# Transposes of two finished tiles in every second step, with three places for keys and x

## The chip, the cores and the metric

The kernel runs on one core of a Trainium2 chip, in one launch. The metric is the device time of one execution in microseconds (us). The kernel before takes 389.77 us, the median of three runs (389.64 to 392.35).

## The reference, cut to what matters

```
# retention attention: batch 8, heads 8, sequence 576, head size 64
scores = q @ k.T / sqrt(64)
Dmat   = where(rel >= 0, gamma[h] ** rel, 0)        # rel = row - column
attn   = (scores * Dmat) @ v
x      = attn, one row a token: 4608 x 512
# mixture of experts on x: 8 experts, hidden size 1024
do     = x @ w_skip > 0
e      = argmax(x[do] @ w_gate);  g = softmax(...)[e]
y      = g * (relu(x @ w1[e]) @ w2[e])              # one expert a token
out    = x;  out[do] = x[do] + y
```

Each token's output is its x, plus the result of one expert where `do` holds.

## The kernel before, in words

The first part of the kernel is a loop over 36 tiles of 128 tokens (`for g in range(NT)`, lines 856 to 888). Nine tiles make a pair of batch entries; the ninth holds the last 64 tokens of both. A tile's q, k, v and a second form of k come as two loads of 512 KB each (`load_half`, on SP's queue), into one of five buffers `u`. The second part (`experts`) runs the experts on gathered rows; it begins with the first lead expert, for which tiles are counted and gathered while the last steps of the loop still run.

The order of TensorE's instructions is the order of the source (a manual schedule for this engine). The other engines' orders are chosen by a planner from its own costs, apart from instructions that are pinned: `tc.keep_in_program_order` holds an instruction behind the one traced before it on its engine.

One step g holds, in this order:

- **Scores** of tile g + 1 (`scores`, line 571), on TensorE tiles of 64x64, and between them the products of masked scores and v of tile g - 1 (`second`, line 662). A tile's scores have two parts: `psc`, the near part, in bank `sc0` or `sc1` by the parity of the tile, and `psq`, the far part, in the one bank `sc2`.
- **Masks** of tile g + 1 (`decay`, lines 586 to 593): one VectorE product for the far part, one for the near part of each half of the partitions, and for each half a ScalarE copy of the rest of the near part. They read the banks and write `sq` and `u`.
- **Keys** of tile g + 2 and **value rows** of tile g + 1 (`keys`, line 601, and `rows_of`, line 623), on GpSimd. The keys `kn` have two places.
- Once in four steps (g = 5, 9, ...) the **gate logits** of four tiles (`logits_a`, line 712), and in the step after it their transposes into bank `xn` (`logits_b`, line 727). VectorE then computes the gates of a group of tiles (`route_a`).
- **State and values** (lines 637 and 686), on TensorE tiles of 128x64. VectorE multiplies the result into `xt` (line 698).
- **Turning a finished tile** (`stage_c`, lines 700 to 707): four transposes of tile g - 2 on TensorE, in tiles of 128x128, into the one bank `xn`; a ScalarE copy to `xn` in SBUF, which has two places; and a DMA to `out`, issued on ScalarE's queue.
- **Routing** (`routing`, line 800): it adds the slot matches of the step before on TensorE (`slot_add`, line 277), and then takes up to three pieces of a list: `route_b` (ranks of a group of tiles; one short set of products, then small VectorE operations) or the slot match of one tile (line 272, VectorE). A piece is due only from a given step. From step 28 up to eight pieces are taken.

Pools give each name a number of places (`bufs`); an instruction that writes a place waits until its last reader is done. The pool `ap` has two unless a call says otherwise.

Of the kernel before, what the change touches and what calls it, by code (L numbers as in the profile page):

```python
# [11 lines left out]
F32 = mybir.dt.float32  # L12
# [5 lines left out]
ALU = mybir.AluOpType  # L18
# [3 lines left out]
B, H, S, D = 8, 8, 576, 64  # L22
NTOK, DM, NE, DF = B * S, H * D, 8, 1024
P = 128
NT = NTOK // P
HALF = S // P * 2
NQ = HALF + 1
NPR = H // 2
# [24 lines left out]
GROUPS = (8, 8, 8, 4, 4, 4)  # L53
KONE = 2
QD = 32
NQD = P // QD
KCUT = 3
KRANK = 4
KFRONT = 1
KCOUNT = 3  # L60
# [27 lines left out]
def kernel(  # L88
# [9 lines left out]
    nc = tc.nc  # L98
# [28 lines left out]
    nc.gpsimd.iota(iota, pattern=[[P, NBLK], [1, P]], base=0, channel_multiplier=0, allow_small_or_imprecise_dtypes=True)  # L127
    desc = const.tile([P, NE], F32, tag="desc", name="desc")
    nc.gpsimd.iota(desc, pattern=[[-1, NE]], base=NE, channel_multiplier=0, allow_small_or_imprecise_dtypes=True)
    pidx = const.tile([P, NT], F32, tag="pidx", name="pidx")  # L130
    nc.gpsimd.iota(pidx, pattern=[[0, NT]], base=0, channel_multiplier=1, allow_small_or_imprecise_dtypes=True)
    tidx = const.tile([P, NT], F32, tag="tidx", name="tidx")
    nc.gpsimd.iota(tidx, pattern=[[1, NT]], base=1, channel_multiplier=0, allow_small_or_imprecise_dtypes=True)
    ones = const.tile([P, P], BF16, tag="ones", name="ones")
# [81 lines left out]
    starts = np.cumsum((0,) + GROUPS).tolist()  # L216
# [4 lines left out]
    def route_b(ps, first, late, pin, n, t0, ex, mb):  # L221
        c0 = NE * NCMP * NBLK + t0 * NE
        pr = ps[:, c0 : c0 + n * NE]

        nc.tensor.matmul(pr, utri, mb, start=first, stop=False, skip_group_check=True)
        if t0:
            nc.tensor.matmul(
                pr, ones, cbs[t0].unsqueeze(1).broadcast_to([P, n, NE]), start=False, stop=False, skip_group_check=True
            )
        for t in range(n - 1):  # L230
            nc.tensor.matmul(
                pr[:, (t + 1) * NE :],
                ones,
                mb[:, t : t + 1, :].broadcast_to([P, n - 1 - t, NE]),
                start=False,
                stop=t == n - 2,
                skip_group_check=True,
            )
        if first:
            nc.vector.tensor_copy(cp[:, :, 1], pidx[:, : max(GROUPS)])  # L240
            tile_numbers(t0, n)
        sm = rt.tile([P, n], F32, tag="sm", name=f"sm_{t0}")
        add = nc.vector.tensor_reduce(sm, ex, axis=AX.X, op=ALU.add)
        if pin:
            tc.keep_in_program_order(add)
        nc.vector.reciprocal(cp[:, :n, 2], sm)
        for k in (2, 3):
            gb = rt.tile([P, n], BF16, tag="gb", name=f"gb_{t0}_{k}")
            nc.vector.tensor_copy(gb, cp[:, :n, k])
            nc.vector.tensor_tensor(cp[:, :n, k + 1], cp[:, :n, k], gb, ALU.subtract)  # L250
        nc.vector.tensor_tensor(
            mc[:, t0 : t0 + n, :].rearrange("p t (e k) -> p t e k", k=NCMP),
            mb.unsqueeze(3).broadcast_to([P, n, NE, NCMP]),
            cp[:, :n].unsqueeze(2).broadcast_to([P, n, NE, NCMP]),
            ALU.mult,
        )
        prv = pr.rearrange("p (t e) -> p t e", e=NE)
        if late:
            nc.vector.tensor_tensor(prv, prv, bump.unsqueeze(1).broadcast_to([P, n, NE]), ALU.add)
        mk = rt.tile([P, n, NE], F32, tag="mk", name=f"mk_{t0}")  # L260
        nc.vector.tensor_tensor(mk, prv, mb, ALU.mult)
        nc.vector.tensor_reduce(trank[:, t0 : t0 + n], mk, axis=AX.X, op=ALU.add)
        if t0 + n < NT:
            tile_numbers(t0 + n, GROUPS[starts.index(t0 + n)])
# [227 lines left out]
    with ExitStack() as actx:  # L492
# [88 lines left out]
        def decay(g):  # L581

            q = first(g)
            near, far = psc_t.pop(g)
            sc_t[g] = ap.tile([P, NPR, D], F32, tag="sq", name=f"sq_{g}", bufs=2 + LAG)
            nc.vector.tensor_tensor(sc_t[g], far, dq_sb[:, g % NQ // 2], ALU.mult)
            for j in range(2):
                h = halves[1 - j]
                nc.vector.tensor_tensor(  # L589
                    u_t[g][h, j, :, :D], near[h, :, :D], mt_sb[h].unsqueeze(1).broadcast_to([D, NPR, D]), ALU.mult  # L590
                )
                if q.stop > D:
                    nc.scalar.copy(u_t[g][h, j, :, D:], near[h, :, D:])  # L593

        def keys(g):
            i = g % NQ
            if i == HALF:
                return
            kn_t[g] = ap.tile([P, NPR, P], F32, tag="kn", name=f"kn_{g}")
            k = TK + i // 2 * 2  # L600
            nc.gpsimd.tensor_tensor(  # L601
                kn_t[g].rearrange("p a (j i) -> p a j i", j=2),
                u_t[g][:, 3].rearrange("p a (j i) -> p a j i", j=2),
                tt_sb[:, k : k + 2, :].rearrange("p j a -> p a j").unsqueeze(3).broadcast_to([P, NPR, 2, D]),
                ALU.mult,
            )
# [93 lines left out]
        def stage_c(g, tag="xn"):  # L700
            b, o = divmod(g, NB)
            px = pp.tile([P, DM], F32, tag=tag, name=f"px_{g}")
            for c in range(NCC):
                nc.tensor.transpose(px[:, c * P : (c + 1) * P], xt_t[b][:, c, o * P : (o + 1) * P], ident)
            xn = ap.tile([P, DM], F32, tag="xn", name=f"xn_{g}")
            nc.scalar.copy(xn.rearrange("t (p c) -> t p c", c=NCC), px.rearrange("t (c p) -> t p c", c=NCC))
            nc.scalar.dma_start(out[g * P : (g + 1) * P, :], xn)

# [147 lines left out]
        for g in range(NT):  # L856
            ahead = g + 1 < NT
            last = g - LAG
            products = [scores(g + 1)] if ahead else []
            if last >= 0 and last % NQ < HALF:  # L860
                products.append(second(last))
            in_turn(*products)
            if g and g + UAHEAD - 1 < NT:
                load_half(g + UAHEAD - 1, 2, last_product())
            if last >= 0 and last % NQ == HALF:
                in_turn(second(last))
            if ahead:
                decay(g + 1)
            if g == 0:
                rows_of(1)  # L870
            if g + 2 < NT:
                keys(g + 2)
            if g and ahead:
                rows_of(g + 1)
            if g + 1 < len(NKEEP):
                keep_up(NKEEP[g + 1])
            if g < NQ - 1 and g % 2 == 0:
                table(g // 2 + 1)
            elif g < NQ - 1:
                growth(g // 2 + 1)  # L880
            logits(g)
            in_turn(state(g), *([values(last)] if last >= 0 else []))
            if g + UAHEAD < NT:
                load_half(g + UAHEAD, 0)
            if last >= 1:
                stage_c(last - 1)
            routing(0 if g == NT - 1 else 3 if g < starts[KCUT + 1] else 8)
            weights()
        g = NT
        if LAG:  # L890
# [520 lines left out]
```

## Time and profile before

| what | value |
|---|---|
| median of three runs | 389.77 us |
| the profiled execution | 392.81 us, span 391.1 us |
| TensorE (PE) busy | 369.3 us, 94% |
| VectorE (DVE) busy | 275.5 us, 70% |
| ScalarE (ACT) busy | 181.4 us, 46% |
| GpSimd (POOL) busy | 149.1 us, 38% |
| moved by DMA | 106.15 MB, mean 271 GB/s |

Busy time is the union of an engine's instructions over the span. TensorE's products are pipelined, so its instructions overlap, and the weight loads (PEld) run beside the products. The loop over tiles lies between some 5 and 152 us. Times within the trace count from the start of the span. A wait is put down to what ended it; "issue" means that nothing that the profile shows ended it.

### The profile page before, as it was taken

How to read it: one execution, taken by the hardware profiler on the slowest of the kernel's cores; microseconds unless marked ns; L12 is line 12 of the kernel's file. 1: busy time of each engine (PE TensorE's matmuls, PEld its weight loads, DVE VectorE, ACT ScalarE, POOL GpSimd, SP SyncE). 2: the span in 40 equal slices, each digit the busy share in tenths (PEclk: the TensorE clock that was granted, in tenths of full speed). 3: DMA queues.
4: the chain of work that ended last, by engine and by line, in shares of the span. 5: the costliest groups of instructions: out<-in, count | busy, mean ns of one | idle time of the engine just before them, and what ended most of it. 6: DMA issues, size and time to landing. Idle time of an engine off the chain costs nothing. (4 is left out here: it accounts for less than half of the span.)

```text
span 391.1 us, 12327 instructions
## 1 busy us (share of the span) xinstructions
PE 369.3 (94%) x4884; PEld 335.0 (86%) x4886; DVE 275.5 (70%) x615; ACT 181.4 (46%) x369; POOL 149.1 (38%) x211
## 2 busy tenths in 40 slices
PE   7889999989998989999999999999999999999992
PEld 3758777777886967888899999999999999999992
DVE  3665688568577886876856767857877877687763
ACT  2444555444544567215544545453645536554311
POOL 5875674564555589451134100520320421002032
PEclk9999999999999999999999999999999999999998
DMA  8997998999899896346896987869979998886511
GB/s 306 405 345 233 385 330 309 321 323 329 288 341 340 293 400 219 129 102 212 287 274 193 355 255 271 295 185 358 255 229 376 270 281 306 272 279 219 160 67 61
DMA packets 49573, 106.15 MB, mean 271 GB/s; under 512 B 6102, under 2 KB 21206, under 8 KB 49511
## 3 DMA queue, kind: packets, MB, share of 16 engines
q1 hardware_dynamic: 40951, 85.81, 65.6%
q0 software_dynamic: 3232, 9.99, 7.9%
q10 hardware_dynamic: 5328, 9.52, 6.4%
q8 instruction: 40, 0.66, 0.7%
q14 instruction: 22, 0.18, 0.1%
HBM read 83.51 MB, written 22.28 MB: 271 GB/s over the span
## 5 line engine op out<-in xcount | busy, mean ns | idle before, releaser
L170 DVE TENSOR_TENSOR wlo_w<-w,whi_w 128x1024 fp32r<-128x1024 f32 x59 | 72.0, 1223 | 36.7 <-ACT whi_w L169 33.7
L169 ACT CAST whi_w<-w 128x1024 fp32r<-128x1024 f32 x59 | 61.8, 1050 | 34.6 <-PE py L464 29.3
L464 PE MATMUL py<-hlo,whi_w 128*128 128x336 f32 (+6 forms) x224 | 67.8, 303 | 0.2 <-DVE hlo L473 0.2
L464 PE MATMUL ph<-xhi,wlo_w 128*128 128x336 f32 (+6 forms) x224 | 67.6, 302 | 0.0
L464 PE MATMUL ph<-xlo,whi_w 128*128 128x336 f32 (+6 forms) x224 | 67.5, 302 | 0.0
L464 PE MATMUL ph<-xhi,whi_w 128*128 128x336 f32 (+6 forms) x224 | 67.5, 301 | 0.0
L464 PE MATMUL py<-hhi,wlo_w 128*128 128x336 f32 (+6 forms) x224 | 67.5, 301 | 0.0
L464 PE MATMUL py<-hhi,whi_w 128*128 128x336 f32 (+6 forms) x224 | 67.4, 301 | 0.0
L1032 POOL DMA_INDIRECT out<-rs,sidx x17 | 21.2, 1247 | 85.5 <-DVE rs L1031 78.8
L601 POOL TENSOR_TENSOR kn<-u,tab_sb 128x512 f32<-128x512 f32 x32 | 34.1, 1067 | 46.1 <-DMA u<-qkv 27.3
L623 POOL TENSOR_TENSOR vs<-u,tab_sb 64x256 f32<-64x256 f32 x72 | 45.2, 628 | 10.6 <-DMA u<-qkv 2.8
L686 PE MATMUL pxt<-u,vs 128*64 128x128 f32 (+1 forms) x576 | 47.8, 269 | 1.2 <-issue 1.1
L589 DVE TENSOR_TENSOR u<-psc,tab_sb 64x256 f32<-64x256 f32 x72 | 30.3, 420 | 24.9 <-PE pxt L662 8.7
L593 ACT COPY u<-psc 64x256 f32<-64x256 f32 x64 | 23.4, 366 | 50.9 <-DVE u L589 46.3
L472 ACT ACTIVATE hhi<-ph 128x336 fp32r<-128x336 f32 (+8 forms) x61 | 25.8, 423 | 43.2 <-PE ph L464 34.8
L464 PEld LDWEIGHTS py<-hlo,whi_w 128*128 128x128 f32 x224 | 42.2, 188 | 0.7 <-DVE hlo L473 0.7
L464 PEld LDWEIGHTS ph<-xhi,whi_w 128*128 128x128 f32 x224 | 42.3, 189 | 0.1
L464 PEld LDWEIGHTS ph<-xlo,whi_w 128*128 128x128 f32 x224 | 42.3, 189 | 0.1
L464 PEld LDWEIGHTS py<-hhi,whi_w 128*128 128x128 f32 x224 | 42.3, 189 | 0.0
L464 PEld LDWEIGHTS ph<-xhi,wlo_w 128*128 128x128 f32 x224 | 42.3, 189 | 0.0
L464 PEld LDWEIGHTS py<-hhi,wlo_w 128*128 128x128 f32 x224 | 42.3, 189 | 0.0
L571 PE MATMUL psc<-u 64*64 64x128 f32 (+1 forms) x576 | 39.9, 272 | 1.3 <-issue 0.9
(213 smaller groups left out, 779.4 us busy)
## 6 DMA issues: line engine op xcount, KB each, us to landing
u<-qkv SPq DMA_DIRECT2D x68, 512.0 KB
w<-w SPq DMA_DIRECT2D x64, 512.0 KB
out<-xn ACTq DMA_DIRECT2D x36, 256.0 KB
hop<-xg SPq DMA_DIRECT2D x12, 256.0 KB
xh<-hop SPq DMA_DIRECT2D x48, 64.0 KB
hopy<-yp SPq DMA_DIRECT2D x24, 128.0 KB
yr<-hopy SPq DMA_DIRECT2D x6, 512.0 KB
u<-qkv SPq DMA_DIRECT2D x4, 256.0 KB
```

Of the source, the lines that this page charges most:

```text
L169: nc.scalar.copy(hi, t)
L170: nc.vector.tensor_tensor(lo, t, hi.bitcast(F32), ALU.subtract)
L464: nc.tensor.matmul(ps, x, y, start=first and n == 0, stop=last and n == 3 * len(terms) - 1)
L472: nc.scalar.activation(hi, ph, AF.Relu)
L571: nc.tensor.matmul(psc_t[g][c][halves[1 - j ^ c], a, : q.stop - q.start], u[halves[j], 1 - j, a, c * D : (c + 1) * D], u[halves[j], j, a, ...
L589: nc.vector.tensor_tensor(u_t[g][h, j, :, :D], near[h, :, :D], mt_sb[h].unsqueeze(1).broadcast_to([D, NPR, D]), ALU.mult)
L593: nc.scalar.copy(u_t[g][h, j, :, D:], near[h, :, D:])
L601: nc.gpsimd.tensor_tensor(kn_t[g].rearrange("p a (j i) -> p a j i", j=2), u_t[g][:, 3].rearrange("p a (j i) -> p a j i", j=2), tt_sb[:, k ...
L623: nc.gpsimd.tensor_tensor(vs_t[g][h, j], u_t[g][h, 2, :, j * D : (j + 1) * D], tt_sb[h, TV + g % NQ // 2, :].unsqueeze(2).broadcast_to([D, ...
L686: nc.tensor.matmul(pxt[halves[j], a, q], vs_t[g][:, j, a, :], u_t[g][:, j, a, q], start=False, stop=a == NPR - 1, skip_group_check=True,)
L1032: done = nc.gpsimd.indirect_dma_start(out=out, out_offset=bass.IndirectOffsetOnAxis(ap=idx, axis=0), in_=rs[:n], in_offset=None, bounds_ch ...
```

## The change

In the steps before step 28, the finished tiles are turned in pairs, in odd steps alone: tile g - 3 by way of bank `xn`, then tile g - 2 by way of bank `sc0`, which is the near scores' bank of the tile whose masks belong to that step (`sc{(g+1)%2}`). Even steps turn none, and route none: routing takes up to four pieces in odd steps. From step 28 all is as before, a tile a step.

The keys and the x copies have three places each. To make room in SBUF, `pidx` has 8 columns and not 36.

All masks are pinned in program order on VectorE. For tiles of even number from 4 to 28 the two near parts come first, one behind the other, and the far part last; for the other tiles the far part comes first. ScalarE's copies are traced behind all of them.

```diff
+NXN = 3
+NKN = 3
...
-    pidx = const.tile([P, NT], F32, tag="pidx", name="pidx")
-    nc.gpsimd.iota(pidx, pattern=[[0, NT]], base=0, channel_multiplier=1, allow_small_or_imprecise_dtypes=True)
+    pidx = const.tile([P, max(GROUPS)], F32, tag="pidx", name="pidx")
+    nc.gpsimd.iota(pidx, pattern=[[0, max(GROUPS)]], base=0, channel_multiplier=1, allow_small_or_imprecise_dtypes=True)
...
-            nc.vector.tensor_tensor(sc_t[g], far, dq_sb[:, g % NQ // 2], ALU.mult)
-            for j in range(2):
-                h = halves[1 - j]
-                nc.vector.tensor_tensor(
-                    u_t[g][h, j, :, :D], near[h, :, :D], mt_sb[h].unsqueeze(1).broadcast_to([D, NPR, D]), ALU.mult
-                )
-                if q.stop > D:
+
+            def far_part():
+                tc.keep_in_program_order(nc.vector.tensor_tensor(sc_t[g], far, dq_sb[:, g % NQ // 2], ALU.mult))
+
+            def near_part():
+                for j in range(2):
+                    h = halves[1 - j]
+                    near_mask = nc.vector.tensor_tensor(
+                        u_t[g][h, j, :, :D], near[h, :, :D], mt_sb[h].unsqueeze(1).broadcast_to([D, NPR, D]), ALU.mult
+                    )
+                    tc.keep_in_program_order(near_mask)
+
+            for part in (near_part, far_part) if g % 2 == 0 and 3 < g <= starts[KCUT + 1] else (far_part, near_part):
+                part()
+            if q.stop > D:
+                for j in range(2):
+                    h = halves[1 - j]
                     nc.scalar.copy(u_t[g][h, j, :, D:], near[h, :, D:])
...
-            kn_t[g] = ap.tile([P, NPR, P], F32, tag="kn", name=f"kn_{g}")
+            kn_t[g] = ap.tile([P, NPR, P], F32, tag="kn", name=f"kn_{g}", bufs=NKN)
...
-            xn = ap.tile([P, DM], F32, tag="xn", name=f"xn_{g}")
+            xn = ap.tile([P, DM], F32, tag="xn", name=f"xn_{g}", bufs=NXN)
...
-            if last >= 1:
+            if g >= starts[KCUT + 1]:
                 stage_c(last - 1)
-            routing(0 if g == NT - 1 else 3 if g < starts[KCUT + 1] else 8)
+                routing(0 if g == NT - 1 else 8)
+            elif last >= 1 and g % 2:
+                stage_c(last - 2)
+                stage_c(last - 1, f"sc{(g + 1) % 2}")
+                routing(4)
```

Here `last` is g - 1 and `starts[KCUT + 1]` is 28.

## Rows read from the trace of the kernel before

**Rows 1.** The page, part 1: busy us (share of the span) and instructions.
```profile
PE 369.3 (94%) x4884; PEld 335.0 (86%) x4886; DVE 275.5 (70%) x615; ACT 181.4 (46%) x369; POOL 149.1 (38%) x211
```

**Rows 2.** Busy time by stretch: steps, end; last granted clock, DMA share, GB/s.
```profile
16.80:116.20 99.40, 92.79 (x2241) 75.67 (x2239) 67.01 (x174) 48.34 (x118) 58.55 (x85) 1.00 0.92 323
...
152.20:391.10 238.90, 231.15 (x1644) 223.88 (x1642) 172.00 (x331) 106.13 (x192) 55.21 (x56) 0.99 0.74 238
```

**Rows 3.** TensorE's waits, 16.8 to 152 us: total us, times, longest us.
```profile
PE psq L571 <- issue: 2.6, 3, 1.6
PE pxt L662 <- issue: 2.2, 3, 1.0
PE pl L712 <- issue: 1.6, 1, 1.6
PE pxt L686 <- issue: 1.1, 1, 1.1
PE pn L727 <- ACT xn L706: 1.0, 2, 0.6
PE psc L571 <- issue: 0.9, 1, 0.9
PE psc L571 <- DMA u<-qkv: 0.2, 1, 0.2
```

**Rows 4.** Waits of SP's queue of loads, 16.8 to 116.2 us.
```profile
SPq L516 <- PE pxt L686: 45.0, 26, 4.3
SPq L516 <- PE pxt L662: 30.9, 22, 2.6
```

**Rows 5.** Timeline of TensorE at 123.7 us: start, us, line, count, idle before.
```profile
123.74 0.27 PE L571 MATMUL psq<-u 64*64 64x64 f32 x1 [1.59 <-issue]
```

**Rows 6.** DMA view, 16.8 to 152 us: queues with packets, MB, share of 16 engines.
```profile
DMA packets 14492, 43.47 MB, mean 321 GB/s; under 512 B 1615, under 2 KB 1615, under 8 KB 14459
...
q10 hardware_dynamic: 4697, 8.57, 16.7%
...
q8 instruction: 24, 0.39, 1.2%
```

**Rows 7.** Timeline of TensorE through one even step, 102.6 to 106 us.
```profile
102.70 0.33 PE L571 MATMUL psc<-u 64*64 64x128 f32 x2
...
103.79 0.34 PE L637 MATMUL ps_s<-u,kn 128*64 128x64 f32 x4
...
104.84 0.29 PE L637 MATMUL ps_s<-u,kn 128*64 128x64 f32 x4
104.96 0.39 PE L686 MATMUL pxt<-u,vs 128*64 128x128 f32 x4
105.28 0.66 PE L704 MATMUL px<-ident,xt 128*128 128x128 f32 x4
105.87 0.27 PE L571 MATMUL psc<-u 64*64 64x64 f32 x2
```

**Rows 8.** Timeline of TensorE: parts of one block of transposes, cut by windows.
```profile
120.42 0.49 PE L704 MATMUL px<-ident,xt 128*128 128x128 f32 x3
...
120.64 0.27 PE L704 MATMUL px<-ident,xt 128*128 128x128 f32 x1
```

**Rows 9.** Timeline of VectorE and ScalarE in the step of rows 7.
```profile
104.35 0.42 DVE L586 TENSOR_TENSOR sq<-psq,dq_sb 128x256 f32<-128x256 f32 x1
...
104.80 0.42 DVE L589 TENSOR_TENSOR u<-psc,tab_sb 64x256 f32<-64x256 f32 x1
...
105.25 0.36 ACT L593 COPY u<-psc 64x256 f32<-64x256 f32 x1 [0.48 <-DVE u L589]
```

**Rows 10.** Timeline of TensorE at 63.3 us.
```profile
63.30 0.66 PE L727 MATMUL pn<-ident,lt 128*128 128x128 f32 x4 [0.58 <-ACT xn L706]
```

**Rows 11.** Waits of GpSimd and ScalarE, 16.8 to 116.2 us.
```profile
POOL kn L601 <- PE ps_s L637: 10.3, 5, 3.4
...
ACT xn L706 <- DMA out<-xn: 1.5, 2, 1.1
```

**Rows 12.** Slot matches: ns shortest, median, longest; first and last start in us.
```profile
L272 DVE TENSOR_SCALAR r<-iota,trank x36: 394/402/414, 59.8 to 165.6; 128x384 bf16<-128x384 f16 x36
```

More of the change, by code (lines that the diff above doesn't have):

```diff
@@ L239, in route_b @@
         if first:
-            nc.vector.tensor_copy(cp[:, :, 1], pidx[:, : max(GROUPS)])
+            nc.vector.tensor_copy(cp[:, :, 1], pidx)
             tile_numbers(t0, n)
```

## The prediction

> **What bounds the kernel now.** I read the page first: TensorE is busy for 94% of the span [rows 1], so what it does or waits for moves the end. Then the stretches: the change touches the steps from 16.8 to 116.2 us (tiles 0 to 25 turned, every mask up to tile 28); there TensorE is busy 92.79 of 99.40 us at a granted clock of 1.00 (the 2.4 GHz level), and the DMA engines show a share of 0.92 [rows 2]. Behind the steps TensorE is busy for 231.15 of 238.90 us: a gain in the steps passes on to the end, if loads and routing keep up, and both are paced by TensorE's steps. Third, what TensorE waited for in the steps. Of 9.6 us in all, 8.4 us are "issue": nine stops that no semaphore ends [rows 3]. Only 1.0 us is a wait for ScalarE's copy of x, 0.6 us of it in the steps that change (the other 0.4 us lies behind them), and 0.2 us a wait for a load. So loads, keys and masks are not what ends TensorE's waits. The loads in turn mostly wait for TensorE to give their buffers back: 45.0 and 30.9 us on the queue of loads [rows 4].
>
> The nine stops stand inside blocks of products. One is the row at 123.74 [rows 5]: in the middle of the scores, 1.59 us without a matmul. Over the steps the instruction queue of the DMA moves 24 packets, 0.39 MB, so 16 KB each [rows 6]. I read a stop as a block of TensorE's code that came late, at the worst of 24 places 1.6 us late.
>
> **The change part by part.**
>
> *Transposes in pairs.* What a block of four transposes costs TensorE is read from the start of it to the start of what follows: 105.28 to 105.87, 0.59 us [rows 7]. Its first one comes 0.32 us after the last group of values (104.96), where the group before it came 0.12 us earlier: TensorE changes from tiles of 128x64 to 128x128, and something is lost there. Four more transposes behind four cost less, as they follow at 0.11 us: three take 0.49 us, the last of them 0.27 us, so (0.49 - 0.27) / 2 [rows 8]. Four of them are 0.44 us. Two blocks cost 2 x 0.59 = 1.18 us before and 0.59 + 0.44 = 1.03 us after: 0.15 us less a pair, provided that scores come behind values, with no transposes between, after the same 0.32 us. No row shows that junction in a full step. Bounds: 0.12 us (no change of tiles at all) makes it 0.35 us a pair; 0.47 us makes the pair worth nothing. I take 0.32, the nearest row, which also ends a block of values. There are 13 pairs (odd steps 3 to 27): 13 x 0.15 = 1.95 us, between 0 and 13 x 0.35 = 4.6 us.
>
> *Their bank.* The second transposes go to the bank of the scores of tile g + 1, and wait for ScalarE's second copy out of it. In the step at 104 that copy starts at 105.25 and takes 0.36, so it ends 0.33 us behind the start of the transposes at 105.28 [rows 9, 7]. The second four start 0.59 us behind the first: 0.26 us of margin. The new order puts both near masks ahead of the far one: the second near mask moves up by one mask, 0.45 us [rows 9], and the margin to 0.7 us. Cost 0; where the cover is gone, TensorE stands for what is missing.
>
> *The wait for x.* The products of the gate logits write the bank of the transposes and once waited 0.58 us for ScalarE's copy, which stood behind a late mask copy [rows 10]. In the even steps, where these products are, there are no transposes now, and the copy of the step before has the scores as cover: 0.6 us less.
>
> *Three places for x.* ScalarE waited 1.5 us in two places for an output to land [rows 11]. With pairs, the second of a pair needs the place of the first of the pair before, two steps earlier, as now. 0.
>
> *Three places for keys.* GpSimd waited 10.3 us in five places for TensorE to give a keys buffer back [rows 11], but TensorE's page of waits has no row for keys in these steps [rows 3]. 0; what would be late next is the second half of the load, which the keys are made from.
>
> *Routing.* It moves from three pieces a step to four in two steps. What goes into a step on VectorE is 0.4 us a slot match [rows 12]; the lists still end before step 28, from which all is as before. The transposes' copies and output DMAs move with them, a step later for half of the tiles, past nothing on SP or GpSimd; on ScalarE's queue two issues follow each other. The masks are now held behind what VectorE was given last, in even steps up to four slot matches, 1.6 us; the next scores, which write the far mask's bank, start 2.6 us behind the scores before them where no transposes lie between (1.09 to the state and values, 1.49 for these [rows 7]). 0.
>
> Sum: 1.95 + 0.6 = 2.5 us off TensorE's own work. Not all of it counts: where a code block is late, TensorE gets there earlier and stands longer. Nine of 24 blocks are late, so I give 9/24 back: 2.5 x 0.375 = 0.9. The sum is **1.6 us less**. The profiled execution took 392.81 us, its span 391.1, so 391.2 for such a one. It lies 3.0 us above the median of 389.77; taken from the median, **388.2 us**.
>
> The Trainium skill, "Runtime: NRT & Kernel Launch", Instruction fetch mechanics, says that the sequencer fetches the next 16 KiB block itself while it executes the current one, and that crossing a boundary is mostly hidden. The block size agrees with the trace's 16 KB [rows 6], the hiding does not in nine places [rows 3]. By that rule nothing would be given back, and the time would be 387.3.
>
> **The rivals.**
>
> *All of it counts*: the nine stops are there for reasons that do not move with TensorE. 389.77 - 2.5 = 387.3. For it: 15 of 24 blocks come in time. Against: a stop that ends with an arrival is not moved by coming to it sooner. What the Trainium skill says above under "Runtime: NRT & Kernel Launch" is this case.
>
> *Stops go as well.* Even steps carry no outputs, so the code comes sooner there; if half of 8.4 us goes and odd steps lose nothing, 2.5 + 4.2 = 6.7 less, 383.1. For it: the outputs take 16.7% of the DMA engines' time in the steps [rows 6]. Against: the same bytes come in the other step.
>
> *The loads take it back.* The loads give nothing if DMA is the pace: 0.92 of it is in use, and a stretch of steps without stops would run into a late load. 389.8. For it: one wait for a load is there already [rows 3]. Against: it is the only one in 135 us, and 0.2 us long.
>
> *Slower: paired outputs hold up code.* Two outputs of 0.26 MB (128 x 512 x 4 bytes) are issued within a microsecond in odd steps. At the 321 GB/s of the steps [rows 6] one more of them is 0.82 us. If it delays the 12 blocks that fall in odd steps by that, each of them late: 12 x 0.82 = 9.8 us, less what even steps get back (half of nine stops, 0.82 each, 3.7 us). 389.77 - 2.5 + 6.1 = 393.4 with the refund and 397.1 without; 395.2 between. It decides from the point where a block comes later than the last instruction before it; nine do now. For it: stops up to 1.6 us beside queues that are 92% full. Against: most blocks come in time next to single outputs.
>
> **How the numbers follow.** The forecast (388.2) gets 0.40, "all of it counts" 0.17, "stops go as well" 0.16, "the loads take it back" 0.16, slower 0.11. One per cent, about what a measurement can tell from no change, is 3.9 us: faster is below 385.9, slower above 393.7. So faster 0.17 (the rival and a tail of the forecast's low bound), slower 0.11, same 0.72. The range: low, it reaches into the faster rival, to 384.0, beyond the forecast's own low bound (4.6 + 0.6 with nothing given back, 384.6); high, past "the loads take it back" to 392.5, since single runs before lie between 389.64 and 392.35. Left out is about half of the faster rival and the slower one, 0.19.
>
> **What would show it.** TensorE's transposes in 13 groups of eight between 20 and 120 us, each pair 1.0 us from its start to the next scores; no row of TensorE waiting for the x copy in the even steps; "issue" waits of TensorE in the steps near 9 us, not 5 or 15. Wrong would be: transposes waiting for ScalarE's copy of u more than a few tenths in all, waits of the scores for loads above 1 us, or stops that differ by several us from 8.4, since that is larger than the whole gain.

## The result and the profile after

The changed kernel takes 393.96 us, the median of 21 runs (389.07 to 398.9); the kernel before takes 390.43 us beside it (21 runs). The ratio is 1.0061 with a 95% interval of 1.0034 to 1.0088: slower by some 2.4 us, where 1.6 us less were forecast. Ratios here and below leave disturbed runs out, so they can differ from the quotient of two medians.

The profiled execution shows little of that. It took 392.55 us (span 390.8), near the span of 391.1 us of before. The page's first part and the two stretches:

```profile
PE 368.0 (94%) x4886; PEld 335.0 (86%) x4886; DVE 276.6 (71%) x615; ACT 180.5 (46%) x369; POOL 150.4 (38%) x211
```
```profile
16.80:116.20 99.40, 91.77 (x2238) 75.63 (x2234) 67.21 (x175) 46.58 (x118) 59.37 (x87) 1.00 0.93 327
152.20:390.80 238.60, 230.19 (x1639) 223.54 (x1639) 172.16 (x330) 105.61 (x190) 56.13 (x56) 0.99 0.73 237
```

TensorE is busy 1.3 us less than before over the span and 1.0 us less in the first stretch [rows 1, 2], and the end has not moved as much. One execution hides the result because stops come and go from run to run: over 16.8 to 152 us, "issue" was 8.4 us in the profile of before [rows 3] and is 3.8 us here, and neither number is the kernel's own (a second profile of each follows below). What is the changed kernel's own is the first row of TensorE's waits from 16.8 to 152 us (total us, times, longest us):

```profile
PE px L716 <- ACT u L605: 3.4, 4, 1.0
PE ps_s L649 <- issue: 1.7, 3, 1.3
...
PE ps_s L649 <- POOL kn L613: 0.8, 1, 0.8
PE px L716 <- DVE lg L740: 0.6, 1, 0.6
...
PE psc L573 <- DMA u<-qkv: 0.5, 1, 0.5
PE pn L739 <- ACT xn L718: 0.5, 1, 0.5
```

Transposes stand four times, 3.4 us, for ScalarE's copy of `u` out of the near scores' bank. No such row was there before [rows 3]. The four places are steps 11, 15, 19 and 27, odd steps all. Step 15 by the timeline of VectorE, ScalarE and TensorE (start, us, engine, line, idle before):

```profile
65.97 0.67 DVE L710 TENSOR_TENSOR xt<-pxt,gt_sb 128x512 f32<-128x512 f32 x1
...
66.56 0.71 DVE L274 TENSOR_SCALAR r<-iota,trank 128x384 bf16<-128x384 f16 x2
...
67.24 0.39 PE L698 MATMUL pxt<-u,vs 128*64 128x128 f32 x4
67.29 0.86 DVE L595 TENSOR_TENSOR u<-psc,tab_sb 64x256 f32<-64x256 f32 x2
67.56 0.66 PE L716 MATMUL px<-ident,xt 128*128 128x128 f32 x4
...
68.23 0.75 ACT L605 COPY u<-psc 64x256 f32<-64x256 f32 x2 [1.62 <-PE px L716]
...
69.03 0.66 PE L716 MATMUL px<-ident,xt 128*128 128x128 f32 x4 [0.81 <-ACT u L605]
```

The scores of the tile are done by 66.0 us. VectorE first finishes `xt` and two slot matches left from earlier steps, so the near masks begin at 67.29. Both copies follow at 68.23, behind both masks, and end at 68.98. The first four transposes start at 67.56, the second four at 69.03: 1.47 us behind them, where they follow after 0.49 us in a pair that doesn't wait. So a wait costs more than its row says. From its start to what follows, this pair takes 1.96 us, and one without a wait, with the same kind of products behind it, 0.93. Worked out in this way, the four waits of 3.4 us cost TensorE 4.3 us.

At the other three places (steps 11, 19 and 27) it is the operations of the gates, not slot matches, that VectorE does ahead of the near masks. Step 19, the longest wait (its second four transposes start at 84.74):

```profile
82.52 0.27 DVE L208 TENSOR_REDUCE cb<-mks 128x8 bf16<-128x64 bf16 x1
...
82.82 0.17 DVE L210 TENSOR_TENSOR cb<-cb,cb 128x8 bf16<-128x8 bf16 x1
83.00 0.86 DVE L595 TENSOR_TENSOR u<-psc,tab_sb 64x256 f32<-64x256 f32 x2
83.06 0.66 PE L716 MATMUL px<-ident,xt 128*128 128x128 f32 x4
```

Where the copies are done in time, a pair goes through as costed:

```profile
101.00 1.09 PE L716 MATMUL px<-ident,xt 128*128 128x128 f32 x8
...
104.50 0.39 PE L698 MATMUL pxt<-u,vs 128*64 128x128 f32 x4
104.82 0.27 PE L573 MATMUL psc<-u 64*64 64x64 f32 x2
```

Eight transposes in one row of 1.09 us, and scores 0.32 us behind the last values of an even step: the junction that no row of before showed costs what was taken for it.

The code's queue has not moved, and the outputs' queue little. Over 16.8 to 152 us (packets, MB, share) they stand beside [rows 6] as

```profile
q10 hardware_dynamic: 4874, 8.88, 18.5%
...
q8 instruction: 24, 0.39, 1.2%
```

### The profile page after: what moved, and what is told of

The parts are those of the page before. It is cut to its first block, busy times and chain, and to the rows that moved or that the text cites. A ratio compares the mean times of both kernels' runs of the same rounds, so it can differ in the third digit from the quotient of the medians.

```text
span 390.8 us, 12339 instructions
## 1 busy us (share of the span) xinstructions
PE 368.0 (94%) x4886; PEld 335.0 (86%) x4886; DVE 276.6 (71%) x615; ACT 180.5 (46%) x369; POOL 150.4 (38%) x211
## 5 line engine op out<-in xcount | busy, mean ns | idle before, releaser
L1048 POOL DMA_INDIRECT out<-rs,sidx x17 | 19.8, 1166 | 85.0 <-DVE rs L1047 83.8
L649 PE MATMUL ps_s<-u,kn 128*64 128x64 f32 x512 | 37.8, 227 | 4.9 <-POOL kn L613 3.2
L649 PEld LDWEIGHTS ps_s<-u,kn 128*64 128x64 f32 x512 | 30.5, 136 | 13.9 <-issue 7.2
```

What stands on the lines that cost most here:

```text
L649: nc.tensor.matmul(ps_s[halves[j], i % 2, a, :], kn_t[g][:, a, j * D : (j + 1) * D], u_t[g][:, 2, a, j * D : (j + 1) * D], start=i == 0 an ...
L1048: done = nc.gpsimd.indirect_dma_start(out=out, out_offset=bass.IndirectOffsetOnAxis(ap=idx, axis=0), in_=rs[:n], in_offset=None, bounds_ch ...
```

## The experiments

Each kernel has its own ratio to the kernel before, from runs on the same chip; kernels told under one heading shared a chip and its runs of the kernel before, unless said otherwise. A table made from the profiles comes last.

### What part of the change costs

Theory M: the new order of the masks is the cause. Its rivals: the pairs, or the places.

Pairs and their routing alone, with the masks and places of before:

```diff
-            if last >= 1:
+            if g >= starts[KCUT + 1]:
                 stage_c(last - 1)
-            routing(0 if g == NT - 1 else 3 if g < starts[KCUT + 1] else 8)
+                routing(0 if g == NT - 1 else 8)
+            elif last >= 1 and g % 2:
+                stage_c(last - 2)
+                stage_c(last - 1, f"sc{(g + 1) % 2}")
+                routing(4)
```

> The kernel before with the pairs of transposes and their routing alone; masks as before, two places for keys and x. Theory M (masks): the changed kernel is slower because the first ScalarE copy out of the scores' bank now waits for both near masks, and the masks stand late on VectorE in odd steps, so that the second four transposes of a pair wait (four waits of 1.0 us in the changed kernel's profile, 4.0 us with one behind the gate logits). With the masks as before the copies run between the masks: waits of the transposes under 1 us in all, and the time is 1 to 2 us below the kernel before. Rival O (outputs): two outputs in one go hold up loads and blocks of code; then this kernel is slower as the whole change is, by 2 to 4 us, with waits for loads or stops without a releaser in place of the waits for ScalarE.

Measured: 392.58 us, ratio 1.0073 (1.0040 to 1.0107).

The places alone (in every kernel with three places of either kind, `pidx` is the short one of the change):

```diff
-            kn_t[g] = ap.tile([P, NPR, P], F32, tag="kn", name=f"kn_{g}")
+            kn_t[g] = ap.tile([P, NPR, P], F32, tag="kn", name=f"kn_{g}", bufs=NKN)
...
-            xn = ap.tile([P, DM], F32, tag="xn", name=f"xn_{g}")
+            xn = ap.tile([P, DM], F32, tag="xn", name=f"xn_{g}", bufs=NXN)
```

> The kernel before with three places for keys and x alone. Theory M: no difference beyond 1 us, as TensorE waited for x once for 0.6 us and never for keys in the steps. Rival O: no difference either. A slowing of 2 us or more would say that keys taken earlier on GpSimd, or the other layout in SBUF, is the cause.

Measured: 392.16 us, ratio 1.0051 (1.0012 to 1.0089).

The masks alone:

```diff
...
+            for part in (near_part, far_part) if g % 2 == 0 and 3 < g <= starts[KCUT + 1] else (far_part, near_part):
+                part()
...
```

> The kernel before with the masks' order and pins alone, and ScalarE's copies traced behind all masks; one block of transposes a step, all in the bank of their own. Theory M: the copies end some 0.4 us later, but the transposes do not use the scores' bank, so 0 to 1 us slower, with no row of transposes waiting for ScalarE's copy of u above a few tenths. Rival O: 0. If this is slower by 2 us or more, the pins cost in themselves, by what they hold up on VectorE.

Measured: 390.09 us, ratio 1.0008 (0.9978 to 1.0037).

Pairs and places together, without the masks (the first two of these diffs):

> The changed kernel with the masks and copies as before: pairs and three places. Theory M: 1 to 2.5 us faster than the kernel before, waits of transposes for ScalarE under 1 us. Rival O: 2 to 4 us slower than the kernel before, as the whole change.

Measured: 394.59 us, ratio 1.0075 (1.0034 to 1.0116).

Theory M fell: the masks alone cost nothing that can be told, and the pairs without them are as slow as the whole. The pairs alone have the changed kernel's wait, at other lines of the source; the pairs with places have less of it (TensorE's waits, 0 to 152 us, of the one and then of the other):

```profile
PE px L704 <- ACT u L593: 2.9, 4, 1.1
PE ps_s L637 <- POOL vs L623: 2.9, 2, 1.6
```
```profile
PE px L706 <- ACT u L595: 1.6, 3, 0.8
```

So theory W took its place: the second four transposes meet ScalarE's late copies, since VectorE has gates and slot matches to do ahead of the masks. Rival O: the outputs, now two close together, hold up code or loads. Pairs with places speak against W as the whole cause: 1.6 us of the wait, and the same 1.0075.

### Taking the wait away, and pairing the outputs alone

The pairs alone, with VectorE's two pieces moved behind the masks (the gates of a group thus a step later):

```diff
...
-            slot_match(t)
+            if g < starts[KCUT + 1]:
+                with tc.issue_after(marks["mask"].ins):
+                    slot_match(t)
+            else:
+                slot_match(t)
...
+            if later:
+                with tc.issue_after(marks["mask"].ins):
+                    route(*later.pop())
             if lt is not None:
                 logits_b(*lt)
-                route(lt[0])
+                if g < starts[KCUT + 1]:
+                    later.append((lt[0], g + 2))
+                else:
+                    route(lt[0])
...
```

> The pairs alone (old masks, old places) with two pieces of VectorE's work moved: the gates of a step are worked out one step later, behind that step's masks, and the slot matches stand behind the masks. Theory W (the second four transposes of a pair wait for ScalarE's copies out of their bank, because VectorE has gates and slot matches to do ahead of the masks): the waits of the transposes for ScalarE, 2.9 us in the pairs alone, fall below 1 us, and the time falls by 2 to 3 us from the 392.6 of the pairs alone, to 389 to 391, ratio to the kernel before 0.997 to 1.003. Rival O (two outputs close behind each other hold up code and loads): the outputs are as close as in the pairs alone, so it is as slow, ratio 1.005 to 1.009, whatever the transposes wait.

Measured: 391.19 us, ratio 1.0027 (0.9990 to 1.0063); TensorE has no wait for ScalarE's copies of `u` any more. Against the pairs alone, which ran on another chip, the ratio is lower by 0.0046, plus or minus 0.0050 (the half-widths joined as roots of squares): in time this run alone doesn't tell W from O.

The kernel before with three places for x and the outputs of two tiles issued together:

```diff
...
+            ready.append((g, xn))
+            if g % 2 or g >= starts[KCUT + 1] - 2:
+                with tc.issue_after(turned.ins):
+                    for t, x in ready:
+                        nc.scalar.dma_start(out[t * P : (t + 1) * P, :], x)
+                ready.clear()
...
```

> The kernel before with three places for x, where the outputs of two tiles are issued together behind the copy of the second, in odd steps; transposes and copies stay single. Rival O: the two outputs together hold up code, 2 to 4 us slower than the kernel before, ratio 1.005 to 1.01. Theory W: nothing beyond what three places for x do by themselves, ratio within 0.002 of the run with these places alone.

Measured: 392.01 us, ratio 1.0023 (0.9987 to 1.0058).

Three places for keys alone, and three for x alone:

```diff
-            kn_t[g] = ap.tile([P, NPR, P], F32, tag="kn", name=f"kn_{g}")
+            kn_t[g] = ap.tile([P, NPR, P], F32, tag="kn", name=f"kn_{g}", bufs=NKN)
```

> The kernel before with three places for keys and nothing else. The three places for keys and x together were slower by 0.5% (0.1 to 0.9). If keys that are made earlier are the cause (GpSimd takes VectorE's port or the loads' halves earlier): ratio 1.003 to 1.007. If the places do nothing (a difference of that size lies in the runs, or comes from x): 0.998 to 1.002.

Measured: 392.43 us, ratio 1.0042 (1.0007 to 1.0076).

```diff
-            xn = ap.tile([P, DM], F32, tag="xn", name=f"xn_{g}")
+            xn = ap.tile([P, DM], F32, tag="xn", name=f"xn_{g}", bufs=NXN)
```

> The kernel before with three places for x and nothing else. ScalarE waited 1.5 us in two places for an output to land; that is off TensorE's path: ratio 0.998 to 1.002. If the places for x made the 0.5% of the two together (outputs that run on later collide with loads): 1.003 to 1.007.

Measured: 390.5 us, ratio 1.0012 (0.9985 to 1.0039).

The wait goes as W says, and the times lean to W without deciding: paired outputs by themselves are within 0.0011 of three places for x, which they contain, but their interval reaches into O's range. The places for keys look slow, but see the next control.

### The whole kernel without the wait, and a control

The kernel before once more, with no difference:

> The kernel before once more, as a kernel of its own: it gives a second profile of it, and shows how far two sets of runs of one program lie apart. All theories: ratio 0.997 to 1.003. If sets of 12 runs differ by more than that without any change, the differences of 0.4 to 0.6% measured so far show nothing.

Measured: 391.88 us, ratio 1.0028 (0.9993 to 1.0064). Nothing was changed, so a single ratio of 1.003 shows nothing, and 1.0042 for the keys little.

The changed kernel once more, with no difference:

> The changed kernel once more, for a second profile and a comparison on the same chip as the next two. Theory W: transposes wait 3 to 4 us for ScalarE and VectorE in odd steps without gate logits, ratio 1.004 to 1.009.

Measured: 394.66 us, ratio 1.0090 (1.0050 to 1.0129).

The changed kernel, whole, with the gates and slot matches behind the masks (the same edit as above, with this one in the new `near_part`):

```diff
-                    near_mask = nc.vector.tensor_tensor(
+                    near_mask = marks["mask"] = nc.vector.tensor_tensor(
```

> The changed kernel, whole, with the gates worked out one step later, behind that step's masks, and the slot matches behind the masks. Theory W (the waits of the transposes for ScalarE cost the gain): these waits fall from 3 to 4 us to below 1 us, and the kernel is 2 to 3 us faster than the changed kernel on the same chip, ratio to the kernel before 0.997 to 1.003. Rival O (the paired transposes, copies and outputs cost it by code, loads or the clock): as slow as the changed kernel within 1 us.

Measured: 391.99 us, ratio 1.0007 (0.9973 to 1.0041).

The same with two places for keys:

```diff
-NKN = 3
...
-            kn_t[g] = ap.tile([P, NPR, P], F32, tag="kn", name=f"kn_{g}", bufs=NKN)
+            kn_t[g] = ap.tile([P, NPR, P], F32, tag="kn", name=f"kn_{g}")
```

> The same with two places for keys, as in the kernel before. Three places for keys alone measured 1.0042 (1.0007 to 1.0076). If that is real, this is another 1 to 1.5 us faster than the one with three, and 1 to 2 us faster than the kernel before, ratio 0.994 to 0.999; if keys' places do nothing, within 0.5 us of the one with three.

Measured: 392.12 us, ratio 0.9986 (0.9940 to 1.0031): 0.0021, or 0.8 us, below the one with three places, plus or minus 0.0057. That is between the two expectations, and the interval holds both: this run decides nothing on the keys.

TensorE's waits from 16.8 to 120 us of the changed kernel's second profile, then of the kernel before's, then of the kernel with late gates:

```profile
PE px L716 <- ACT u L605: 2.6, 4, 0.8
PE pl L724 <- issue: 1.7, 1, 1.7
PE psq L573 <- issue: 1.6, 2, 1.4
```
```profile
PE pxt L662 <- issue: 1.6, 2, 1.3
PE pn L727 <- ACT xn L706: 1.3, 1, 1.3
```
```profile
PE pxt L698 <- issue: 1.9, 1, 1.9
...
PE px L716 <- ACT u L605: 0.2, 1, 0.2
```

On one chip and against the same runs, late gates take the ratio from 1.0090 to 1.0007. The difference is 0.0083, and with the two half-widths (0.0040 and 0.0034) joined as roots of squares, plus or minus 0.0052: 3.2 us, 1.2 to 5.3. Rival O, by which the time stays within 1 us, doesn't hold for this part of the loss. Step 15 of that kernel shows how (the gates' and slot work now follows the masks):

```profile
65.83 0.86 DVE L595 TENSOR_TENSOR u<-psc,tab_sb 64x256 f32<-64x256 f32 x2
```
```profile
66.75 0.66 PE L716 MATMUL px<-ident,xt 128*128 128x128 f32 x4
66.77 0.74 ACT L605 COPY u<-psc 64x256 f32<-64x256 f32 x2 [0.98 <-issue]
...
67.57 0.66 PE L716 MATMUL px<-ident,xt 128*128 128x128 f32 x4 [0.17 <-ACT u L605]
```

The near masks begin 0.9 us ahead of the transposes, where in the changed kernel they began 0.3 us ahead of them, and the second four wait 0.17 us, not 0.81.

### Is it the wait, or do late gates help any kernel?

The late gates in the kernel before (the edit as above, transposes single):

> The kernel before with the gates worked out one step later, behind that step's masks, and the slot matches behind the masks; transposes single as ever. Theory W: no transposes of this kernel wait for the near bank, so there is nothing to win: ratio 0.998 to 1.003. Rival L (late gates help any version by 2 to 3 us): ratio 0.992 to 0.995.

Measured: 390.17 us, ratio 0.9999 (0.9972 to 1.0027). Late gates by themselves are worth nothing that can be told; they are worth 3.2 us where transposes wait behind the masks.

The other direction, in the kernel with late gates: the near masks of five tiles worked out twice.

```diff
             for part in (near_part, far_part) if g % 2 == 0 and 3 < g <= starts[KCUT + 1] else (far_part, near_part):
+                if part is near_part and g % 4 == 0 and 12 <= g <= starts[KCUT + 1]:
+                    near_part()
                 part()
```

> The changed kernel with late gates, in which the near masks of tiles 12, 16, 20, 24 and 28 are worked out twice over (same inputs, same outputs), so that ScalarE's copies come about 0.9 us later in five odd steps that have a pair of transposes. Theory W: the transposes wait again, 0.5 to 0.9 us in five places, 2.5 to 4.5 us in all, and the time is 2 to 4 us above the kernel with late gates (ratio to the kernel before 1.0007): 1.005 to 1.011. Rival L: VectorE's time ahead of the masks costs nothing, ratio 0.998 to 1.004.

Measured: 396.17 us (6 runs), ratio 1.0181 (1.0127 to 1.0236). And in the kernel before:

```diff
-                nc.vector.tensor_tensor(
+                for _ in range(2 if g % 4 == 0 and 12 <= g <= starts[KCUT + 1] else 1):
+                    nc.vector.tensor_tensor(
```

> The kernel before with the near masks of the same five tiles worked out twice over. Theory W: its transposes don't use the near bank, and the next scores into it come a step later, so at most the far bank is given back late: 0 to 1 us, ratio 0.998 to 1.003. If late masks cost any version the same: 2 to 4 us, ratio 1.005 to 1.011.

Measured: 391.88 us (9 runs), ratio 1.0070 (1.0028 to 1.0112).

The doubled masks in the kernel with pairs, step 15, and its row of waits from 16.8 to 120 us:

```profile
66.56 1.78 DVE L595 TENSOR_TENSOR u<-psc,tab_sb 64x256 f32<-64x256 f32 x4
...
68.42 0.74 ACT L607 COPY u<-psc 64x256 f32<-64x256 f32 x2 [1.93 <-PE px L718]
...
69.22 0.66 PE L718 MATMUL px<-ident,xt 128*128 128x128 f32 x4 [1.11 <-ACT u L607]
```
```profile
PE px L718 <- ACT u L607: 3.0, 4, 1.1
```

The wait is back in four of the five places (steps 11, 15, 19 and 27), 0.5 to 1.1 us each, with nothing of the gates' order touched. The time rises by more than the wait: 0.0174 over the kernel with late gates, some 6.8 us, against 0.0070 where transposes are single. The extra masks cost something in either kernel, more than was expected; the part that only pairs feel is 0.0104, plus or minus 0.0077 (three half-widths joined in the same way), 4.1 us. The trace, of the fastest of the six runs (392.33 us), accounts for 3.0 of that.

Pairs only in every fourth step, where they had not waited:

```diff
+                if g % 4 == 1:
+                    stage_c(last - 2)
+                    stage_c(last - 1, f"sc{(g + 1) % 2}")
+                elif g % 4:
+                    stage_c(last - 1)
```

> The pairs alone, with pairs only in every fourth step (5, 9, ... 25), where they did not wait; the tiles of the other pairs are turned singly in their own steps. Theory W: waits of the transposes for ScalarE's copies of u below 0.5 us; 6 or 7 pairs save at most 1 us: ratio 0.996 to 1.002, about 2 us faster than the pairs alone (1.0073). If the pairs themselves cost time (their outputs, copies or code), half of what the pairs alone cost: 1.003 to 1.005.

Measured: 395.4 us (6 runs), ratio 1.0104 (1.0033 to 1.0176). A miss. No transposes wait for `u`, but another wait took the place (TensorE's first row, 16.8 to 152 us, and the step at 65 us):

```profile
PE px L704 <- DVE lg L728: 2.3, 3, 1.1
```
```profile
63.69 1.05 DVE L272 TENSOR_SCALAR r<-iota,trank 128x384 bf16<-128x384 f16 x3
...
65.12 0.29 DVE L728 TENSOR_REDUCE lg<-pn 128x36 f32<-128x144 f32 x1
...
65.46 0.66 PE L704 MATMUL px<-ident,xt 128*128 128x128 f32 x4 [1.12 <-DVE lg L728]
```

Single transposes of an even step share bank `xn` with the gate logits, whose sum on VectorE now stood behind slot matches of the odd step.

### The routing alone, and what is left without pairs

```diff
-            routing(0 if g == NT - 1 else 3 if g < starts[KCUT + 1] else 8)
+            if g >= starts[KCUT + 1]:
+                routing(0 if g == NT - 1 else 8)
+            elif g % 2:
+                routing(4)
```

> The kernel before with routing in odd steps alone, up to four pieces, and single transposes in every step. If the slot matches of an odd step push VectorE's sum of the gate logits back in the next even step, the transposes wait for it as in the run with half of the pairs: 2 to 2.5 us in three places, ratio 1.004 to 1.008. Theory W alone (only pairs have a wait to meet): no such waits, ratio 0.998 to 1.003.

Measured: 390.82 us, ratio 1.0002 (0.9967 to 1.0036), with 2.1 us of waits of transposes for that sum in its profile. So the routing does make that wait, and by itself it does not show in the time; the 1.0104 of half of the pairs stays unexplained. Its rows come from a run of 391.53 us, 3.9 us below the median of its six, and so show little of what made the others slow.

The kernel before with the new masks and late gates, no pairs (the edits of the masks and of late gates as above):

> The kernel before with the new order of the masks and with late gates, single transposes, two places each. The order of the masks alone measured 1.0008 (0.9978 to 1.0037), the late gates alone 0.9999 (0.9972 to 1.0027). Theory W: neither has a wait of TensorE to take away, ratio 0.996 to 1.002. If both give the 0.5 to 0.9 us that they show at equal mean clock, 0.994 to 0.997.

Measured: 391.01 us, ratio 0.9999 (0.9960 to 1.0038). No version beats the kernel before by what can be told.

### All profiles together

From the first scores of tile 3 to the first scores of tile 28, TensorE's time is split into waits of over 0.15 us and the rest. Means in us, over profiles; the eight with single transposes are the kernel before (two), the masks, paired outputs, keys' and x places, late gates, and late gates with masks; the four with pairs are the changed kernel (two), the pairs alone, and pairs with places; the three with late gates are those above. The profiles of places for both, of routing alone, of half of the pairs and of doubled masks are left out.

| | elapsed | rest | waits | transposes for `u` or sums | gate logits for x | GpSimd | issue |
|---|---|---|---|---|---|---|---|
| single, 8 | 97.9 | 92.2 (91.75 to 92.80) | 5.7 (4.5 to 7.6) | 0 | 1.1 | 1.2 | 3.3 |
| pairs, 4 | 99.9 | 90.7 (89.34 to 91.76) | 9.2 (8.1 to 10.2) | 1.9 (0.7 to 2.7) | 0 | 2.4 | 4.7 |
| pairs, late gates, 3 | 98.1 | 91.3 (90.78 to 91.95) | 6.8 (4.9 to 8.6) | 0.1 | 0 | 1.9 | 4.3 |

The pairs do save: 1.5 us of the rest, and 1.1 us of the logits' waits. They pay 1.9 us at the bank, 1.2 us more to GpSimd and 1.4 us more in stops: 2.0 us slower in this stretch. The 1.4 us hang on where the stretch ends: from 16.8 to 152 us "issue" is 5.7, 5.8 and 5.7 us in the three rows (single ones 3.9 to 8.4), so the pairs are not shown to make more stops. In the last row two of three profiles have a stretch at half clock in the rest (below), so 91.3 is high; without the slowest of the three (two places for keys, 394.2 us) the row reads 96.9, 90.9, 6.0, 0.1, 0, 1.7, 3.9.

## Why the prediction was wrong

**The step that failed is "Their bank", costed at 0.** It read a margin of 0.26 us off one even step of the trace of before [rows 9, 7], added 0.45 us because the second near mask moves up, and took it that the margin would stand after the change. In the changed kernel none of this stood. Measured: 3.4 and 2.6 us of waits in two profiles, the sign of being wrong that the prediction itself had named, and 3.2 us of time (1.2 to 5.3) when VectorE's gates and slot matches go behind the masks.

Would the odd steps, in which pairs stand, have told more? Two of them in the trace of before, by the copies of `u` and the transposes:

```profile
59.77 1.37 DVE L272 TENSOR_SCALAR r<-iota,trank 128x384 bf16<-128x384 f16 x4
...
60.12 0.66 PE L704 MATMUL px<-ident,xt 128*128 128x128 f32 x4
...
61.62 0.36 ACT L593 COPY u<-psc 64x256 f32<-64x256 f32 x1 [1.49 <-DVE u L589]
```
```profile
67.38 0.43 DVE L589 TENSOR_TENSOR u<-psc,tab_sb 64x256 f32<-64x256 f32 x1 [0.82 <-PE pxt L662]
...
68.73 0.37 ACT L593 COPY u<-psc 64x256 f32<-64x256 f32 x1 [0.48 <-DVE u L589]
68.77 0.66 PE L704 MATMUL px<-ident,xt 128*128 128x128 f32 x4
```

At 60.12 (step 13) the second copy ends 1.86 us behind the start of the transposes: second transposes 0.59 us later would have stood 1.27 us. At 68.77 (step 15) it ends 0.33 us behind, the 0.26 us of margin again. Worked out in the same way, the odd steps of before have margins from 1.1 us (step 5) to minus 1.3 us (step 13, where four slot matches stood ahead of the second near mask). But the two below zero, steps 13 and 21, do not wait in the changed kernel, and the four that wait, 11, 15, 19 and 27, have 0.2, 0.3, 0.6 and 0.1 us there (0.0, 0.3, minus 0.4 and 0.0 in the second profile of before). So the odd steps warned that the margin is thin; where the waits would come they did not tell.

What changed is how far ahead of the step's first transposes the near masks begin. In step 15 it was 1.39 us (67.38, 68.77), after 0.82 us in which VectorE was idle; in the changed kernel it is 0.27 us (67.29, 67.56), right behind two slot matches. The four steps, in us, one profile each:

| step | before | routing alone | pairs alone | changed |
|---|---|---|---|---|
| 11 | 1.36 | 0.97 | 0.38 | 0.25 |
| 15 | 1.39 | 1.39 | 0.90 | 0.27 |
| 19 | 1.72 | 0.59 | 0.00 | 0.05 |
| 27 | 1.32 | 0.86 | 0.58 | 0.61 |

The change itself makes the masks late. Routing in odd steps takes part of the lead in three of the four, and the pairs take 0.3 to 0.6 us more, which fits the 0.59 us that TensorE no longer spends on transposes in the even step before: it comes to the pair sooner, and VectorE does not. That share is read from single profiles (in the second one of before, step 19 has 0.74); no run took it apart.

The 0.45 us did not come: at 68.73 the second copy ends 1.72 us behind the start of the first near mask (67.38), and in the changed kernel both end 1.69 us behind it (67.29 to 68.98), since the first copy too now waits for both masks. And the second four transposes follow the first after 0.49 us, not 0.59, as the prediction's own 0.11 us a transpose would have told: 0.1 us less of margin everywhere.

**"Routing", costed at 0, named the delay and sent it to the wrong place.** It saw masks held behind VectorE's last slot matches, and tested only whether the next scores would notice. The transposes behind the same copies were the ones that did. It counted slot matches alone; at three of the four waits the gates' operations stand there.

**What was given back (0.9 us for late code) is not decided.** That a stop is a block of code that came late was the prediction's reading, and the traces bear it out: all nine stops of before [rows 3] end 1.31 to 1.50 us behind the end of a 16 KB transfer on the code's queue, and so (1.2 to 1.6 us) do 115 of 139 stops of over 0.2 us in all 20 profiles from 16.8 to 152 us, though such a transfer comes only once in 5.6 us. But their sum is the same with pairs and without, 5.8 and 5.7 us, and spreads from 3.7 to 8.4 us over the profiles of the table, far more than 0.9. GpSimd's waits, which the prediction put at nothing, rise by 1.2 us in the table. The Trainium skill, "Runtime: NRT & Kernel Launch", Instruction fetch mechanics, holds that crossing a block is mostly hidden; in the profile of before 15 of 24 blocks agree with that, and nine do not.

**Right:** the price of a pair (1.03 us to the next scores forecast, 1.02 us measured in the changed kernel where nothing waits; 1.95 us forecast for all 13, 1.5 us measured in the rest, where single profiles differ by 1 us and more); the scores behind values at 0.32 us; the logits' wait for x (0.6 us forecast, 1.1 us measured in the table); x places at 0 (ratio 1.0012, not told from 1). Places for keys at 0 is neither shown wrong nor right: 1.0042 alone, no difference that can be told in the whole kernel with late gates.

**The rivals.** "Paired outputs hold up code" came out on the right side (395.2 against 393.96) but its reason is not borne out: outputs issued in pairs alone give 1.0023, against 1.0012 for their places, and the stops' sum does not rise. "All of it counts" and the forecast failed alike with the bank; what of their gain counts is not told. "Stops go as well" looked right in the first profile (3.8 us for 8.4 us); in the second profiles, from 0 to 152 us, the changed kernel has 7.5 us of "issue" and the kernel before 5.9. "The loads take it back" has no more waits of scores for loads than the kernel before in the second profiles, 1.1 us in each.

**What stays open.** The bank's 3.2 us are most of the 4 us between forecast and result, not all. With late gates the bank's wait is gone, TensorE's own work is shorter, and the time is that of the kernel before (1.0007), not 1.6 us below it (0.9960). GpSimd's waits (0.7 us more in the table) and a lower clock (below) may hold it; no run singled one out. Pairs with places (1.0075 with 1.6 us of the wait), half of the pairs (1.0104) and the full price of doubled masks are not explained by their rows.

## What to carry to other kernels

When work is moved into another engine's buffer, read the margin in every step in which it will stand there, and then ask what the change does to it: which engine now comes sooner, and what the third engine does first. Here the near masks' lead in the four steps that waited fell by 0.7 to 1.7 us, and the thin margins of before were gone. One profile of a kernel whose stops differ by 3 us from run to run can't show a change of 2 us; profiles of unchanged twins tell the change's own waits from the others.

## What was not expected of the hardware

A long stop can cost twice. Three stretches of the kernel with late gates, around a stop of 1.9 us that ends at 43.3 us (busy times of TensorE, its weight loads, VectorE, ScalarE, GpSimd, then granted clock, DMA share, GB/s):

```profile
40.00:43.50 3.50, 1.59 (x36) 1.09 (x32) 0.14 (x1) 1.10 (x3) 1.83 (x5) 1.00 1.04 408
43.50:46.90 3.40, 3.40 (x52) 3.01 (x52) 0.69 (x1) 1.90 (x4) 2.40 (x4) 0.50 0.81 280
46.90:50.30 3.40, 3.40 (x102) 2.98 (x94) 2.18 (x5) 1.43 (x4) 1.66 (x3) 1.00 0.83 301
```

TensorE is busy 1.59 of 3.50 us; then the granted clock is 0.50, the 1.2 GHz level, for 3.4 us, and TensorE does 52 matmuls where it does 102 in the 3.4 us behind, at the 2.4 GHz level. In the 20 profiles of this case there are seven such falls ahead of the kernel's end. Six came less than 2 us behind the end of a stop, the seventh as a stop ended (1.45, 1.59, 1.72, 1.80, 1.91, 2.07 and 2.43 us long). A stop does not always have a fall behind it: 18 others of 1.45 us or more had none, one of them 2.72 us long.

Over the runs that the ratios rest on, the mean granted clock was 0.9944 for the changed kernel and 0.9952 for the kernel before; by a straight line through all of these runs, each kernel's mean taken out, 0.001 of clock goes with 0.33 us, so some 0.3 us of the loss goes with the clock. That the waits at the bank make it fall is not shown: with late gates, where they are gone, it was 0.9928 and 0.9941, lower still.
